# Attention, routed experts and SiLU layer on one core: PSUM as tiles of single banks, opened stage by stage, and one VectorE addition moved ahead of a transpose

## The chip, the cores and the metric

The kernel runs on one core of one Trainium2 chip. The core has five engines that each work through their own list of instructions: TensorE (matrix products, PE in the profile, with PEld for its weight loads), VectorE (DVE), ScalarE (ACT), GpSimd (POOL) and SyncE (SP, which issues transfers here). They wait for one another by semaphores. TensorE writes its products to PSUM, an accumulator memory of eight banks, each 512 float32 numbers on each of 128 partitions; VectorE and ScalarE read them from there. The metric is the time of one execution in microseconds (us) on the device, the median of several runs.

## The reference

Three layers follow one another; the output of each is the input of the next.

```python
# attention without softmax, B, S, D = 8, 3072, 256; z has 64 columns
scores = (1 / S) * np.matmul(z, z.transpose(0, 2, 1))
attn = np.maximum(scores, 0.0) ** 2
x = (u * np.matmul(attn, v)).reshape(B * S, D)
# routed experts: each of the 24576 tokens goes to one of E = 8
logits = normalized(x) @ normalized(expert_emb).T / tau
expert_idx = np.argmax(logits, axis=1)
out[mask_e] = gate_w[mask_e, None] * (np.maximum(x[mask_e] @ w1[e], 0) @ w2[e])
# the last layer, 256 -> 2048 -> 256
h = out @ w_in
return (h * (1 / (1 + np.exp(-h)))) @ w_out
```

## The kernel before

All products are made of float32 numbers cut into a high and a low part, so that one product of the reference is three matmuls here (high by high, high by low, low by high). The program is written out instruction by instruction in the order in which each engine executes it; nothing reorders it later. The semaphore waits are put in by the framework: an instruction that writes a tile waits for those that read it before.

**Stage A, the attention, with the router of the experts.** `pipeline_ab` runs over units g. A unit is a 512 by 256 piece of the scores. In the round of unit g TensorE makes the scores of unit g+2 (tile `s`), adds unit g to the output sums (`acc`), and then, since the scores are symmetric, adds a transposed copy of unit g-2 to the sums of another row block: `emit_T_a` makes that product in a bank of the tile `acct`, and one round later `flush_a` adds it on VectorE to the token rows `xg` (line 707). The tile `acct` has two banks; `ps_bank` hands them out in turn, to these transposed sums and also to the router, which makes its logits there (matmuls of lines 500 and 502). VectorE transposes the logits out of the bank (`raw`, line 507, tile `rt`) and adds their two parts (line 509). Jobs listed under `pre` run at the beginning of a round, `raw` among them; `bg` in its middle, `post` at its end.

**Stage B, the experts.** The same loop goes on with rounds of the experts' products; `ps_s` gives the two-bank tiles `s0` and `s1` in turn.

**Stage C, the last layer.** `pipeline_c` goes over 24 blocks of 1024 tokens (b) and in each over 8 groups of hidden columns (i), 192 iterations g = 8 b + i and one to drain. The first product is done by a Winograd form of Strassen's scheme: seven products M1 to M7, of three matmuls each (lines 1207 to 1209), give the four quadrants H11, H12, H21, H22. They go through four banks: `Q`, one of the two banks of the tile `m0` in turn, and `R` and `Z`, the two banks of the tile `m1`. M1 begins in Q, and M6, M5 and M3 are added onto it; M2 is made in R; M7 begins in Z and M4 is added onto it. Between two of these, ScalarE copies Q (`copy`, line 1264) or VectorE adds R or Z to a copy (`add`, line 1267, tile `hs`). ScalarE makes the sigmoid (`sig`, line 1270, tile `sg`), VectorE multiplies by it (`mul`, line 1273), ScalarE rounds the result (line 1279, tile `g`), and VectorE subtracts for the low part (line 1283). The multiplication for H12 reads Q itself, and is the last to read it: its row is `sg<-m,sg`. One iteration later TensorE multiplies the four quadrants by `w_out` into four banks `acc` (lines 1233 to 1235, two pairs of three matmuls for each quadrant, which makes 24 in an iteration). TensorE's order in an iteration is M1, M2, the H11 of the iteration before, M6, M7, H22, M5, H21, M3, M4, H12.

Between M7 and the subtraction for H11 comes what is to be done for the next block, one step for each i (`prep_c`): i=1 loads it, i=2 transposes, i=3 and 4 subtract, i=5, 6 and 7 cut 128x1024 numbers into parts (`split`: ScalarE line 151, VectorE line 152, tile `xp`), and i=0 cuts the last 128x512. In i=0 VectorE also takes the four finished `acc` of the block before out of PSUM (`evac_c`, line 1241).

Of the kernel before, what the change touches and what calls it, by code (L numbers as in the profile page):

```python
# [8 lines left out]
F32 = mybir.dt.float32  # L9
# [6 lines left out]
PSUM = bass.MemoryType.PSUM  # L16
# [4 lines left out]
def relu2_attention__moe_top1__silu_ffn_kernel(  # L21
# [24 lines left out]
    P = 128  # L46
# [34 lines left out]
    CH = CB // 2  # L81
# [3 lines left out]

    const = ctx.enter_context(tc.tile_pool(name="const", bufs=1))
    small = ctx.enter_context(tc.tile_pool(name="small", bufs=2))
    psS = ctx.enter_context(tc.tile_pool(name="psS", bufs=1, space=PSUM))
    psA = ctx.enter_context(tc.tile_pool(name="psA", bufs=4, space=PSUM))
    main = ctx.enter_context(tc.tile_pool(name="main", bufs=1))  # L90
    only_a = ExitStack()
    poolA = only_a.enter_context(tc.tile_pool(name="poolA", bufs=1))
# [14 lines left out]
    def pt(tag, shape, dtype, name, bufs):  # L107
        return poolA.tile(shape, dtype, tag=tag, name=name, bufs=bufs)
# [3 lines left out]
    sp_state = dict(n=0, bank=0, acct=None)  # L112

    def ps_s(shape, name):
        n = 0
        if sp_state["acct"] is None:
            n = sp_state["n"] % 2
            sp_state["n"] += 1
        return psS.tile(shape, F32, tag=f"s{n}", name=name, bufs=1)

    def ps_bank(n, name):

        if sp_state["acct"] is None:
            return ps_s([P, n], name)
        sp_state["bank"] ^= 1
        return sp_state["acct"][:, sp_state["bank"], 0:n]

    XS = nc.dram_tensor("xs_scratch", (E * CAP, XW), F32, kind="Internal").ap()
    X2 = nc.dram_tensor("x2_scratch", (N, D), F32, kind="Internal").ap()
# [92 lines left out]
    pre, bg, post = {}, {}, {}  # L222
# [10 lines left out]
    def run(tasks, g):  # L233
        for fn in tasks.pop(g, ()):
            fn()
# [38 lines left out]
    def both(g):  # L274

        return 0 <= g < NIT and UNITS[g][1] != UNITS[g][2]
# [4 lines left out]
    def start_a():  # L281

        for tag, n in (("tl", 1), ("vb", 2 * (NCH - 4)), ("xt0", 1), ("xt1", 1), ("xgh", 1), ("xgl", 1)):
            for _ in range(n):
                pt(tag, [P, 1024], F32, "place", n)
        sp_state["acct"] = psS.tile([P, 2, 512], F32, tag="s1", name="acct", bufs=1)
        low["zr"] = mt("w2", [P, 2, QN // 32, 32], F32, "zr", 4)

    jobs = []
# [386 lines left out]
    def th_a(g):  # L676
        h = TH[g] = (mt("y", [P, 8, 4, 32], F32R, "th", 1 - low["n"]) if g == NIT - 3
                     else mt("xh", [P, 8, 4, 32], F32R, "th"))
        A.activation(out=h, in_=TA[g].rearrange("p i k r -> p k i r"), func=AF.Copy)  # L679
# [24 lines left out]
    def flush_a(g):  # L704
        b, J, I, hf, _, _ = UNITS[g]
        x = XG[b, I][:, 2 * hf:2 * hf + 2, 0:D]
        V.tensor_tensor(out=x, in0=x, in1=TACC.pop(g), op=ALU.add)  # L707
# [248 lines left out]
    for b in range(NBLK):  # L956
        g = NIT + b * FP
# [9 lines left out]
    cw = {}  # L967
# [132 lines left out]
    def pipeline_ab():  # L1100

        g = min(bg)
        while g < NAB or bg:
            ahead = g + 2 if 0 <= g + 2 < NAB else None
            if g == NIT + 1:
                sp_state.update(acct=None, n=1)
            s = rest = None
            if ahead is not None:
                s = (emit_S_a if ahead < NIT else emit_S_b)(ahead)
            run(pre, g)  # L1110
            if both(g - 3):
                flush_a(g - 3)
            if both(g - 1):
                th_a(g - 1)
                tl_a(g - 1)
            if both(g + 1):
                ta_a(g + 1)
            run(bg, g)
            assert g not in pre
            if 0 <= g < NAB:  # L1120
                (emit_AV_a if g < NIT else emit_AV_b)(g)
            if both(g - 2):
                emit_T_a(g - 2)
            if s is not None:
                rest = (elem_a if ahead < NIT else elem_b)(ahead, s)
            if 0 <= g < NIT:
                if ahead >= NIT:
                    evac_a(g, range(QT))
                if rest:
                    rest()  # L1130
                run(post, g)
            else:
                run(post, g)
                if NIT <= g < NAB:
                    evac_b(g)
                if rest:
                    rest()
            g += 1
# [73 lines left out]
    quads, acc_c, out_c, room = {}, {}, {}, {}  # L1212
# [8 lines left out]
    def emit_AV_c(g, q):  # L1221

        b, i = divmod(g, GP)
        f, t = QUADS[q]
        x = quads.pop((g, q))
        start = i == 0 and q in ("H11", "H22")
        stop = i == GP - 1 and q in ("H21", "H12")
        for d in range(2):
            if start:
                acc_c[b, d, t] = psA.tile([P, CH], F32, tag="acc", name="acc")  # L1230
            o = acc_c[b, d, t]
            wh, wl = (cw["o"][:, f * GP + i, y, d * P:(d + 1) * P] for y in range(2))
            T.matmul(o, lhsT=wh, rhs=x[:, 0], start=start, stop=False)  # L1233
            T.matmul(o, lhsT=wh, rhs=x[:, 1], start=False, stop=False)  # L1234
            T.matmul(o, lhsT=wl, rhs=x[:, 0], start=False, stop=stop)  # L1235
# [11 lines left out]
                             in_=o[32 * i:32 * i + 32])  # L1247

    def pipeline_c():
        s0 = psS.tile([P, 2, CH], F32, tag="s0", name="m0", bufs=1)  # L1250
        s1 = psS.tile([P, 2, CH], F32, tag="s1", name="m1", bufs=1)
        ns = NCB * GP
        rooms_c()
        n_quad = 0
        H, C, S = room["H"], room["c"], room["a"]
        for g in range(ns + 1):
            now, old = g < ns, g > 0
            b, i = divmod(g, GP)
            end = old and i == 0
            todo = prep_c(b)[GP] if now and i == 0 else prep_c(b + 1)[i] if now and b + 1 < NCB else []  # L1260
            Q, R, Z = s0[:, g % 2], s1[:, 0], s1[:, 1]

            def copy(n, src):
                A.activation(out=C[n], in_=src, func=AF.Copy)

            def add(q, n, src):
                V.tensor_tensor(out=H[q], in0=src, in1=C[n], op=ALU.add)  # L1267

            def sig(q, src=None):
                A.activation(out=S[q], in_=H[q] if src is None else src, func=AF.Sigmoid)  # L1270

            def mul(q, src=None):
                V.tensor_tensor(out=S[q], in0=H[q] if src is None else src, in1=S[q], op=ALU.mult)  # L1273

            def high(g, q):
                nonlocal n_quad
                quads[g, q] = mt("hl"[n_quad % 2], [P, 2, CH], F32R, "g")
                n_quad += 1
                A.activation(out=quads[g, q][:, 0], in_=S[q], func=AF.Copy)  # L1279

            def low_part(g, q):
                x = quads[g, q]
                V.tensor_tensor(out=x[:, 1], in0=S[q], in1=x[:, 0].bitcast(F32), op=ALU.subtract)  # L1283

            if now:
                emit_M(g, "M1", Q)
            if old:
                high(g - 1, "H12")
                low_part(g - 1, "H22")
            if now:  # L1290
                copy(0, Q)
                emit_M(g, "M2", R)
            if old:
                low_part(g - 1, "H12")
                mul("H21")
                high(g - 1, "H21")
            if now:
                add("H11", 0, R)
            if old:
                low_part(g - 1, "H21")  # L1300
                emit_AV_c(g - 1, "H11")
            if now:
                sig("H11")
                mul("H11")
                emit_M(g, "M6", Q, False)
                copy(1, Q)
                high(g, "H11")
                emit_M(g, "M7", Z)
            for fn in todo:
                fn()  # L1310
            if now:
                low_part(g, "H11")
            if old:
                emit_AV_c(g - 1, "H22")
            if now:
                emit_M(g, "M5", Q, False)
                copy(2, Q)
            if old:
                emit_AV_c(g - 1, "H21")
            if now:  # L1320
                add("H22", 2, Z)
                sig("H22")
                emit_M(g, "M3", Q, False)
                emit_M(g, "M4", Z, False)
            if end:
                evac_c(b - 1, 0, 0)
            if now:
                sig("H12", Q)
                mul("H22")
                high(g, "H22")  # L1330
            if end:
                evac_c(b - 1, 0, 1)
            if now:
                add("H21", 1, Z)
                mul("H12", Q)
                sig("H21")
            if old:
                emit_AV_c(g - 1, "H12")
            if end:
                for d in range(2):  # L1340
                    evac_c(b - 1, 1, d)
# [51 lines left out]
```

## Time and profile before

| | before |
|---|---|
| median of 3 runs | 5296.63 us (5295.66 to 5301.29) |
| profiled execution | 5294.56 us |
| its span, first to last instruction | 5292.8 us |
| TensorE busy in it | 5180.2 us, 98% |
| VectorE busy | 4019.0 us, 76% |
| ScalarE busy | 3501.1 us, 66% |

Stage A takes the first 2055 us or so, stage B lasts to about 3190, stage C to the end. The profile is of one execution. A busy time is the time in which an instruction of that engine is drawn; since matmuls overlap one another, the rows of TensorE are longer than the distance from one to the next, and it is the distance that tells its rate.

### The profile page before, as it was taken

The numbers are of one execution on the slowest core, as the hardware profiler recorded it, in microseconds if no ns is written. First come the engines' busy times: TensorE is split into PE (matmuls) and PEld (weight loads), VectorE is DVE, ScalarE is ACT, GpSimd is POOL, SyncE is SP. The second block draws the span as 40 slices with busy tenths as digits, with TensorE's granted clock in tenths as the row PEclk, the third lists the DMA queues.
The fourth block names the chain that finished last, engine by engine and source line by source line (L and its number), as shares of the span: only waits on it lengthen the run. The fifth ranks groups of instructions, "written<-read, shape, count | busy, mean of one in ns | idle before, by whom it ended". The sixth has DMA issues, their size and how long they took to land.

```text
span 5292.8 us, 76091 instructions
## 1 busy us (share of the span) xinstructions
PE 5180.2 (98%) x27488; PEld 4389.7 (83%) x27488; DVE 4019.0 (76%) x5760; ACT 3501.1 (66%) x5213; POOL 750.0 (14%) x977
## 2 busy tenths in 40 slices
PE   8999999999999999999999998999999999999999
PEld 7889888898989898888888886777777777777777
DVE  6687777777777778788877676777777777777776
ACT  7777777777777776555555555666666666666665
POOL 1131313222222222211111110000000000000000
PEclk9999999999999999999999998999999999999999
DMA  4555565656565656755555551101101010101010
GB/s 148 176 169 181 169 184 163 186 160 183 169 178 169 180 172 185 196 159 160 160 147 160 152 170 41 33 20 29 29 20 32 17 32 17 32 17 32 17 32 17
DMA packets 789371, 594.31 MB, mean 112 GB/s; under 512 B 473692, under 2 KB 706175, under 8 KB 788992
## 3 DMA queue, kind: packets, MB, share of 16 engines
q1 hardware_dynamic: 616960, 464.93, 29.7%
q10 hardware_dynamic: 152928, 73.95, 5.4%
q0 software_dynamic: 19104, 50.56, 2.6%
q8 instruction: 215, 3.52, 0.3%
q14 instruction: 164, 1.34, 0.1%
HBM read 368.03 MB, written 210.73 MB: 109 GB/s over the span
## 4 chain that ended last, share of the span: by engine, by line
PE 65%; issue 11%; DVE 9%; ACT 6%; DMA 6%; POOL 1%; SPq 1%; ACTq 0%; POOLq 0%; DVEq 0%
PE acc L242 6%; PE acc L239 6%; PE m L1207 5%; PE m L1209 4%; PE m L1208 4%; PE acc L1234 4%; PE acc L1233 4%; PE acc L1235 4%; PE acct L700 4%; PE acct L701 4%; PE acct L702 4%; PE acc L241 3%; PE acc L240 3%; PE s L645 2%; PE s L646 2%
## 5 line engine op out<-in xcount | busy, mean ns | idle before, releaser
L1233 PE MATMUL acc<-g,wo 128*128 128x512 f32 x1536 | 598.9, 390 | 0.0
L1234 PE MATMUL acc<-g,wo 128*128 128x512 f32 x1536 | 598.2, 389 | 0.2 <-DVE g L1283 0.2
L1235 PE MATMUL acc<-g,wo 128*128 128x512 f32 x1536 | 597.7, 389 | 0.0
L1279 ACT ACTIVATE g<-sg 128x512 fp32r<-128x512 f32 x768 | 484.1, 630 | 133.2 <-DVE sg L1273 120.2
L1283 DVE TENSOR_TENSOR g<-sg,g 128x512 fp32r<-128x512 f32 x768 | 524.4, 685 | 59.1 <-ACT g L1279 23.9
L700 PE MATMUL acct<-vs,th 128*128 128x256 f32 x1920 | 542.6, 283 | 15.3 <-DVE xg L707 14.4
L701 PE MATMUL acct<-vs,th 128*128 128x256 f32 x1920 | 541.8, 282 | 0.0
L702 PE MATMUL acct<-vs,tl 128*128 128x256 f32 x1920 | 541.4, 282 | 0.0
L242 PE MATMUL acc<-vs,ah 128*128 128x512 f32 x1344 | 533.5, 397 | 0.0
L239 PE MATMUL acc<-vs,ah 128*128 128x512 f32 x1344 | 533.1, 397 | 0.0
L1270 ACT ACTIVATE sg<-hs 128x512 f32<-128x512 f32 x576 | 364.2, 632 | 202.6 <-DVE hs L1267 194.0
L667 DVE TENSOR_TENSOR al<-a,ah 128x1024 fp32r<-128x1024 f32 x336 | 406.2, 1209 | 109.8 <-ACT ah L660 105.0
L1273 DVE TENSOR_TENSOR sg<-hs,sg 128x512 f32<-128x512 f32 x576 | 395.9, 687 | 120.9 <-ACT sg L1270 118.7
L654 ACT ACTIVATE a<-s 128x1024 f32<-128x1024 f32 x336 | 342.5, 1019 | 183.1 <-PE s L646 164.2
L930 ACT ACTIVATE hh<-hps 128x1024 fp32r<-128x1024 f32 (+1 forms) x220 | 213.9, 972 | 336.6 <-PE hps L916 289.3
L931 DVE SCALAR_TENSOR_TENSOR hl<-hps,hh 128x1024 fp32r<-128x1024 f32 (+1 forms) x220 | 254.1, 1155 | 204.9 <-ACT hh L930 202.2
L679 ACT ACTIVATE th<-at 128x1024 fp32r<-128x1024 f32 x240 | 253.4, 1056 | 230.7 <-PE acct L701 130.2
L665 DVE STREAM_TRANSPOSE tb<-a 128x1024 f32<-128x1024 f32 x240 | 297.5, 1240 | 133.1 <-ACT a L656 130.3
L700 PEld LDWEIGHTS acct<-vs,th 128*128 128x128 f32 x1920 | 364.9, 190 | 18.8 <-DVE xg L707 17.6
L241 PE MATMUL acc<-vs,al 128*128 128x256 f32 x1344 | 375.4, 279 | 0.0
L701 PEld LDWEIGHTS acct<-vs,th 128*128 128x128 f32 x1920 | 365.6, 190 | 10.2
L240 PE MATMUL acc<-vs,al 128*128 128x256 f32 x1344 | 374.1, 278 | 0.0
(246 smaller groups left out, 14006.1 us busy)
## 6 DMA issues: line engine op xcount, KB each, us to landing
ts_scratch<-tb SPq DMA_DIRECT2D x240, 512.0 KB
at<-ts_scratch SPq DMA_DIRECT2D x960, 128.0 KB
r<-in_moe_w_dram SPq DMA_DIRECT2D x220, 512.0 KB
vr<-in_v_dram ACTq DMA_DIRECT2D x48, 512.0 KB
ut<-in_u_dram ACTq DMA_DIRECT2D x48, 512.0 KB
xb<-xs_scratch SPq DMA_DIRECT2D x192, 128.0 KB
xc<-x_scratch SPq DMA_DIRECT2D x192, 128.0 KB
out_dram<-oc SPq DMA_DIRECT2D x192, 128.0 KB
```

Source lines behind the costliest of these rows:

```text
L239: T.matmul(acc, lhsT=hs[0], rhs=ws[0], start=start, stop=False)
L240: T.matmul(acc[:, D:2 * D], lhsT=ls[0], rhs=ws[0][:, 0:D], start=False, stop=False)
L241: T.matmul(acc[:, D:2 * D], lhsT=ls[1], rhs=ws[1][:, 0:D], start=False, stop=False)
L242: T.matmul(acc, lhsT=hs[1], rhs=ws[1], start=False, stop=stop)
L700: T.matmul(acc[:, kk], lhsT=lh, rhs=vq[:, 0], start=(q == 0), stop=False)
L701: T.matmul(acc[:, kk], lhsT=lh, rhs=vq[:, 1], start=False, stop=False)
L702: T.matmul(acc[:, kk], lhsT=ll, rhs=vq[:, 0], start=False, stop=(q == QT - 1))
L1233: T.matmul(o, lhsT=wh, rhs=x[:, 0], start=start, stop=False)
L1234: T.matmul(o, lhsT=wh, rhs=x[:, 1], start=False, stop=False)
L1235: T.matmul(o, lhsT=wl, rhs=x[:, 0], start=False, stop=stop)
L1279: A.activation(out=quads[g, q][:, 0], in_=S[q], func=AF.Copy)
L1283: V.tensor_tensor(out=x[:, 1], in0=S[q], in1=x[:, 0].bitcast(F32), op=ALU.subtract)
```

## The change

PSUM's pools are opened and closed with the stages. In stage A the two banks of the transposed sums are two tiles `t0` and `t1` of one bank each; at the beginning of stage B they are given up and the two-bank tile `s1` is opened in a pool of its own; at the beginning of stage C all of these are closed and eight tiles of one bank each are opened, four (`m0` to `m3`) for Q twice, R and Z, and four for the output sums, with a fixed name for each. In the attention's round, the addition `flush_a` is issued ahead of the jobs in `pre`. The diff, whole:

```diff
--- before.py
+++ after.py
@@ -85,8 +85,10 @@
 
     const = ctx.enter_context(tc.tile_pool(name="const", bufs=1))
     small = ctx.enter_context(tc.tile_pool(name="small", bufs=2))
-    psS = ctx.enter_context(tc.tile_pool(name="psS", bufs=1, space=PSUM))
-    psA = ctx.enter_context(tc.tile_pool(name="psA", bufs=4, space=PSUM))
+    not_c, in_a = ExitStack(), ExitStack()
+    psS = not_c.enter_context(tc.tile_pool(name="psS", bufs=1, space=PSUM))
+    psA = not_c.enter_context(tc.tile_pool(name="psA", bufs=4, space=PSUM))
+    psT = in_a.enter_context(tc.tile_pool(name="psT", bufs=1, space=PSUM))
     main = ctx.enter_context(tc.tile_pool(name="main", bufs=1))
     only_a = ExitStack()
     poolA = only_a.enter_context(tc.tile_pool(name="poolA", bufs=1))
@@ -116,14 +118,14 @@
         if sp_state["acct"] is None:
             n = sp_state["n"] % 2
             sp_state["n"] += 1
-        return psS.tile(shape, F32, tag=f"s{n}", name=name, bufs=1)
+        return (sp_state["psB"] if n else psS).tile(shape, F32, tag=f"s{n}", name=name, bufs=1)
 
     def ps_bank(n, name):
 
         if sp_state["acct"] is None:
             return ps_s([P, n], name)
         sp_state["bank"] ^= 1
-        return sp_state["acct"][:, sp_state["bank"], 0:n]
+        return sp_state["acct"][sp_state["bank"]][:, 0:n]
 
     XS = nc.dram_tensor("xs_scratch", (E * CAP, XW), F32, kind="Internal").ap()
     X2 = nc.dram_tensor("x2_scratch", (N, D), F32, kind="Internal").ap()
@@ -283,7 +285,7 @@
         for tag, n in (("tl", 1), ("vb", 2 * (NCH - 4)), ("xt0", 1), ("xt1", 1), ("xgh", 1), ("xgl", 1)):
             for _ in range(n):
                 pt(tag, [P, 1024], F32, "place", n)
-        sp_state["acct"] = psS.tile([P, 2, 512], F32, tag="s1", name="acct", bufs=1)
+        sp_state["acct"] = [psT.tile([P, 512], F32, tag=f"t{i}", name="acct", bufs=1) for i in range(2)]
         low["zr"] = mt("w2", [P, 2, QN // 32, 32], F32, "zr", 4)
 
     jobs = []
@@ -1103,13 +1105,15 @@
         while g < NAB or bg:
             ahead = g + 2 if 0 <= g + 2 < NAB else None
             if g == NIT + 1:
-                sp_state.update(acct=None, n=1)
+                in_a.close()
+                psB = not_c.enter_context(tc.tile_pool(name="psB", bufs=1, space=PSUM))
+                sp_state.update(acct=None, n=1, psB=psB)
             s = rest = None
             if ahead is not None:
                 s = (emit_S_a if ahead < NIT else emit_S_b)(ahead)
-            run(pre, g)
             if both(g - 3):
                 flush_a(g - 3)
+            run(pre, g)
             if both(g - 1):
                 th_a(g - 1)
                 tl_a(g - 1)
@@ -1227,7 +1231,7 @@
         stop = i == GP - 1 and q in ("H21", "H12")
         for d in range(2):
             if start:
-                acc_c[b, d, t] = psA.tile([P, CH], F32, tag="acc", name="acc")
+                acc_c[b, d, t] = cw["ps"].tile([P, CH], F32, tag=f"acc{2 * t + d}", name="acc", bufs=1)
             o = acc_c[b, d, t]
             wh, wl = (cw["o"][:, f * GP + i, y, d * P:(d + 1) * P] for y in range(2))
             T.matmul(o, lhsT=wh, rhs=x[:, 0], start=start, stop=False)
@@ -1247,8 +1251,9 @@
                              in_=o[32 * i:32 * i + 32])
 
     def pipeline_c():
-        s0 = psS.tile([P, 2, CH], F32, tag="s0", name="m0", bufs=1)
-        s1 = psS.tile([P, 2, CH], F32, tag="s1", name="m1", bufs=1)
+        not_c.close()
+        ps = cw["ps"] = ctx.enter_context(tc.tile_pool(name="psC", bufs=1, space=PSUM))
+        banks = [ps.tile([P, CH], F32, tag=f"m{i}", name="m", bufs=1) for i in range(4)]
         ns = NCB * GP
         rooms_c()
         n_quad = 0
@@ -1258,7 +1263,7 @@
             b, i = divmod(g, GP)
             end = old and i == 0
             todo = prep_c(b)[GP] if now and i == 0 else prep_c(b + 1)[i] if now and b + 1 < NCB else []
-            Q, R, Z = s0[:, g % 2], s1[:, 0], s1[:, 1]
+            Q, R, Z = banks[g % 2], banks[2], banks[3]
 
             def copy(n, src):
                 A.activation(out=C[n], in_=src, func=AF.Copy)
```

Line numbers after the change are higher by 2 in the attention and by 4 in stage C. On each of the five engines the instructions are as many as before and, apart from 15 places on VectorE, in the same order. Three places show what moves.

VectorE in the attention, where the router's logits have just been made; `xg<-xg,acct` is the addition of `flush_a`, `rt` and `raw` are the router's. Before:

```order
L667 TENSOR_TENSOR al<-a,ah 128x1024 [waits Activation_49]
L507 STREAM_TRANSPOSE rt<-acct 128x256 [waits PE_49]
L509 TENSOR_TENSOR raw<-rt 128x64 [waits DVE_49]
L707 TENSOR_TENSOR xg<-xg,acct 128x2x256
L684 TENSOR_TENSOR tl<-at,th 128x1024 [waits DMAHW4_49,DMAHW3_49,DMAHW7_49,DMAHW1_49,Activation_49]
```

and after:

```order
L669 TENSOR_TENSOR al<-a,ah 128x1024 [waits Activation_49]
L709 TENSOR_TENSOR xg<-xg,acct 128x2x256 [waits PE_49]
L509 STREAM_TRANSPOSE rt<-acct 128x256 [waits PE_49]
L511 TENSOR_TENSOR raw<-rt 128x64 [waits DVE_49]
L686 TENSOR_TENSOR tl<-at,th 128x1024 [waits DMAHW4_49,DMAHW3_49,DMAHW7_49,DMAHW1_49,Activation_49]
```

The addition stands ahead of the router's two instructions. This is so at 15 places.

TensorE in stage C, at the end of one iteration and the beginning of the next, where M1 (three matmuls) and M2 are made; before, they write `m0` and `m1`:

```order
L1235 MATMUL acc_35801<-g_35839,wo_24236 128x512
L1207 MATMUL m0_35698<-xp_35678,wih_24234 128x512 [waits DVE_49]
L1208 MATMUL m0_35698<-xp_35679,wih_24234 128x512
L1209 MATMUL m0_35698<-xp_35678,wil_24235 128x512
L1207 MATMUL m1_35699<-xp_35678,wih_24234 128x512
L1208 MATMUL m1_35699<-xp_35679,wih_24234 128x512
L1209 MATMUL m1_35699<-xp_35678,wil_24235 128x512
```

and after, two tiles of one bank each, both named `m`:

```order
L1239 MATMUL acc_35817<-g_35855,wo_24244 128x512
L1211 MATMUL m_35713<-xp_35686,wih_24242 128x512
L1212 MATMUL m_35713<-xp_35687,wih_24242 128x512
L1213 MATMUL m_35713<-xp_35686,wil_24243 128x512
L1211 MATMUL m_35714<-xp_35686,wih_24242 128x512
L1212 MATMUL m_35714<-xp_35687,wih_24242 128x512
L1213 MATMUL m_35714<-xp_35686,wil_24243 128x512
```

The order is the same; the wait for VectorE at M1 is gone. M7 and M4 have one before and after.

TensorE at an early transposed sum of the attention, behind the output sums of the round. Before:

```order
L241 MATMUL acc<-vs,al 128x256
L242 MATMUL acc<-vs,ah 128x512
L700 MATMUL acct<-vs,th 128x256 [waits DVE_49]
L701 MATMUL acct<-vs,th 128x256
L702 MATMUL acct<-vs,tl 128x256
```

and after:

```order
L243 MATMUL acc<-vs,al 128x256
L244 MATMUL acc<-vs,ah 128x512
L702 MATMUL acct<-vs,th 128x256
L703 MATMUL acct<-vs,th 128x256
L704 MATMUL acct<-vs,tl 128x256
```

Here too only a wait for VectorE is gone. At 101 of the 240 transposed sums the first matmul no longer has one.

## Rows read from the trace of the kernel before

**Rows 1.** The page, busy us of each engine (share of the span) and its instructions.

```profile
PE 5180.2 (98%) x27488; PEld 4389.7 (83%) x27488; DVE 4019.0 (76%) x5760; ACT 3501.1 (66%) x5213; POOL 750.0 (14%) x977
```

**Rows 2.** TensorE's waits: line <- released by: us in total, times, longest us.

```profile
PE m L1207 <- DVE sg L1273: 32.1, 93, 1.4
...
PE acct L700 <- DVE xg L707: 14.4, 10, 1.8
...
PE acct L500 <- DVE xg L707: 2.1, 1, 2.1
```

**Rows 3.** Windows: us, busy us of PE, PEld, DVE, ACT, POOL; granted clock; DMA share, GB/s.

```profile
3301.00:5259.00 1958.00, 1925.85 (x8192) 1516.37 (x8190) 1526.02 (x2317) 1266.45 (x2093) 0.00 (x0) 1.00 0.10 25
2060.00:3190.00 1130.00, 1126.17 (x5888) 963.58 (x5887) 861.97 (x1275) 619.71 (x961) 245.49 (x240) 1.00 0.57 163
3215.00:3222.00 7.00, 5.67 (x12) 3.52 (x13) 4.83 (x7) 3.36 (x7) 0.00 (x0) 0.50 0.37 84
```

**Rows 4.** Timeline of TensorE, one block: M1s, and in i=2 M6 and H12.

```profile
4334.31 0.50 PE L1207 MATMUL m<-xp,wih 128*128 128x512 f32 x1 [0.25 <-DVE sg L1273]
...
4345.38 0.50 PE L1207 MATMUL m<-xp,wih 128*128 128x512 f32 x1 [0.58 <-DVE sg L1273]
...
4356.10 0.50 PE L1207 MATMUL m<-xp,wih 128*128 128x512 f32 x1
...
4358.97 0.39 PE L1207 MATMUL m<-xp,s 128*128 128x512 f32 x1
...
4365.09 0.39 PE L1233 MATMUL acc<-g,wo 128*128 128x512 f32 x1
...
4387.69 0.50 PE L1207 MATMUL m<-xp,wih 128*128 128x512 f32 x1
...
4398.59 0.50 PE L1207 MATMUL m<-xp,wih 128*128 128x512 f32 x1 [0.25 <-DVE sg L1273]
...
4420.40 0.50 PE L1207 MATMUL m<-xp,wih 128*128 128x512 f32 x1 [0.26 <-DVE sg L1273]
```

**Rows 5.** Timeline of three engines in i=6 of the same block.

```profile
4397.86 0.68 DVE L1273 TENSOR_TENSOR sg<-m,sg 128x512 f32<-128x512 f32 x1
...
4401.84 0.68 DVE L1273 TENSOR_TENSOR sg<-hs,sg 128x512 f32<-128x512 f32 x1
...
4402.32 0.60 ACT L1264 ACTIVATE c<-m 128x512 f32<-128x512 f32 x1 [0.52 <-PE m L1209]
4402.82 0.62 ACT L1279 ACTIVATE g<-sg 128x512 fp32r<-128x512 f32 x1
4403.34 1.05 ACT L151 ACTIVATE xp<-xs 128x1024 fp32r<-128x1024 f32 x1
...
4406.17 0.68 DVE L1267 TENSOR_TENSOR hs<-m,hs 128x512 f32<-128x512 f32 x1
...
4406.91 0.50 PE L1207 MATMUL m<-xp,wih 128*128 128x512 f32 x1
...
4408.76 0.68 DVE L1273 TENSOR_TENSOR sg<-m,sg 128x512 f32<-128x512 f32 x1
```

**Rows 6.** Timeline of VectorE and TensorE at two places of the attention.

```profile
259.01 0.44 DVE L507 STREAM_TRANSPOSE rt<-acct 128x256 f32<-128x256 f32 x1
259.48 0.91 DVE L509 TENSOR_TENSOR raw<-rt 128x64 f32<-128x64 f32 x1
260.32 0.67 DVE L707 TENSOR_TENSOR xg<-xg,acct 128x512 f32<-128x512 f32 x1
...
261.04 0.38 PE L700 MATMUL acct<-vs,th 128*128 128x256 f32 x1 [1.57 <-DVE xg L707]
...
808.93 0.39 PE L700 MATMUL acct<-vs,th 128*128 128x256 f32 x1 [1.84 <-DVE xg L707]
```

**Rows 7.** Timeline of TensorE near the beginning of stage C.

```profile
3209.21 0.63 PE L1207 MATMUL m<-xp,wih 128*128 128x512 f32 x1
3209.63 0.63 PE L1208 MATMUL m<-xp,wih 128*128 128x512 f32 x1
```

## The prediction

> **What bounds the kernel now.** I read the page's busy shares first. TensorE is busy for 5180.2 of 5292.8 us [rows 1], so whatever the change does to the time it must do through TensorE, and only about 2% looks free. That share hides something, because a matmul held back by a semaphore is drawn longer, not idle. So I went on to TensorE's waits. The longest group is the first matmul of a product in the last stage (stage C), waiting for a VectorE multiplication `sg`; in the attention, the transposed sums wait for VectorE's addition to `xg` ten times [rows 2].
>
> Then I put the stages side by side [rows 3]. The middle stage has matmuls for 1126.17 of 1130 us. The steady part of stage C, from 3301 to 5259 us, has 8192 matmul records in 1958.00 us, 0.239 us each. What one costs when nothing holds it is seen inside an iteration: from the first matmul of M6 at 4358.97 to the first of the `H12` pair at 4365.09 there are 27 matmuls in 6.12 us, 0.2267 us each [rows 4]. An iteration has 45 matmuls (seven products of 3, eight of the output side of 3), so it would take 10.20 us; 1958.00 over 8192/45 = 182 iterations is 10.76. TensorE loses 0.56 us in each, 106 us in 192, though its row says 98% busy.
>
> Where it loses them: M1, the first product. It writes bank g%2 of the tile `m0`, whose last reader is two iterations back. Yet it starts at 4398.59, 0.05 us after the multiplication `sg<-m` of the iteration before (4397.86 + 0.68 = 4398.54), which reads the other bank [rows 4, 5]. So the wait is for the whole two-bank tile. Held this way, the matmul is drawn with 0.50 us instead of 0.39: the next one starts 0.11 us later than usual, which is a second price of every hold [rows 4].
>
> **The change part by part.** *Single-bank tiles in stage C.* M1 loses its wait on VectorE in 191 of 192 iterations, as the order of the program shows; M7 now waits for the last reader of its own bank, an addition of the iteration before, and no longer for one in `m1`'s other half. Instruction counts and orders stay as they are on all five engines except for VectorE's swap below, so no duration changes; only what is waited for does. What M1 gives up must be checked against what is late next. VectorE and ScalarE keep up with the rate on average (1526 and 1266 us busy in the 1958 [rows 3]), but M4 adds onto the bank that the addition `hs<-m,hs` has just read, and keeps that wait.
>
> I take a block of eight iterations, one block of tokens, from M1 to M1 [rows 4]: i=0 (four evacuations of `acc`) 4334.31 to 4345.38, 11.07 us; i=1 10.72; i=2 to 4 31.59 for three; i=5 10.90; i=6 and 7 21.81. In all 86.09.
> - i=0 and i=2 to 4: M4 there is not late now (i=2: its 27 undisturbed matmuls above contain M4). Without the hold at M1 they run at TensorE's own 10.20.
> - i=1: here M7 is late as well, behind the evacuations on VectorE. That wait is the other-bank kind and goes too; the evacuations still push ScalarE's copies towards M5. Nothing shows how far, from 0 up to what an ordinary iteration loses, 0.33. I take 0.15, near the middle: 10.35.
> - i=5 to 7 prepare the next block: ScalarE rounds 128x1024 and VectorE subtracts, between the copy of M6 and the addition that M4 waits for. [Rows 5] show the chain in i=6. From multiplication to multiplication (`sg<-m`, 4397.86 to 4408.76) it takes 10.90 us, and I followed it link by link: `sg<-hs` ends at 4402.52; ScalarE copies M6 (`c<-m` 4402.32) and so starts `g` only at 4402.82; `xp` on ScalarE, then on VectorE `xp`, `g` and `hs<-m,hs` to 4406.85, M4 at 4406.91. M4 is barely late now (0.03, and 0.11 for the hold). All links but one are VectorE's and ScalarE's own. The one is the copy, which is tied to TensorE: with TensorE ahead it lies earlier, and `g` can follow the multiplication by the 0.05 us or so that hand-overs here take, at 4402.57, 0.25 earlier. The chain is then 10.65 us against TensorE's 10.20. So in i=6 and 7 most of what M1 gave up **comes back at M4**, and the iteration takes 10.66; in i=5 TensorE comes out of ordinary iterations with VectorE's lag small, and M4 loses what it loses now: 10.20 + 0.14 = 10.34.
>
> Sum: 10.20 + 10.35 + 30.60 + 10.34 + 21.32 = 82.81, against 86.09: 3.28 a block, 78.7 in 24 blocks. The last block prepares nothing and gains 8 x 0.33 = 2.6 instead, and the first iterations run at the lower clock [rows 7], where TensorE is slower than VectorE's chain: I take off 1.7 for both, the second by choice. **Stage C: -77 us.** Its bounds: 0 if the hold stays, 106 if no wait is left.
>
> *Single-bank tiles and the swap in the attention.* Ten holds of the transposed sums come to 14.4 us, one of the router's sums to 2.1 [rows 2]. Seven of the ten look like the one at 261.04 [rows 6]: VectorE does the transpose `rt` (259.01), the addition `raw` (259.48, 0.91 long) and only then the addition to `xg` (260.32), and TensorE, which has been waiting for 1.57 us, goes on 0.05 after it. In the changed order the addition to `xg` comes first. But at this place the router has used one of the two banks in between, so the sum goes to the bank that `rt` reads. It then waits for 0.67 + 0.44 from 259.01, to about 260.17: 0.87 is won, 6.1 us in seven. The other three (808.93 is the longest, 1.84 [rows 6]) wait for an addition that reads the other bank; they go, 3.4 us together, and so does the router's 2.1, each with its 0.11. **Attention: -12 us**, bounds 0 (ScalarE, whose reads TensorE waits for at other places, takes it back) and 18 (all of it). Moving `rt` and `raw` behind one addition of 0.67 us delays the routing by that much, 15 times; nothing on TensorE waits for `raw` within its iteration. VectorE's new waits for TensorE at `xgl` and `bb` name reads and sums that their data always needed, and cost nothing. Opening pools anew costs no instruction; the waits at the two stage borders are for the same last readers as before.
>
> The sum is made against the profiled execution, 5294.56 us with 1.76 us around its span: 5294.6 - 77 - 12 = 5205.6. The runs' median is 2.1 above that execution; I put 1.4 on it: **5207 us**.
>
> **Rivals.**
> - *Nothing comes back.* Perfetto Trace Analysis, the Trainium skill's page, section Optimizing Tensor Performance, asks that independent groups of matmuls rotate through different PSUM banks, so that reading one out overlaps the next group; by it, all of the wait should go. M1, M2 and M7 then are such groups, M4 is not. Time if M4's holds also went: 5294.6 - 106 - 12 = 5177. For it: the chain in [rows 5] has ScalarE steps that could close up further. Against it: M4 adds onto a bank that VectorE must have read.
> - *More comes back.* If the chain of VectorE and ScalarE binds in all eight iterations, each wins only the 0.25 of the copy: 48 us, and half of the attention's: 5294.6 - 48 - 6 = 5241. Against it: in an ordinary iteration VectorE and ScalarE have no preparation to do.
> - *Slower: the clock.* With the holds moved, TensorE could be granted its lower level in stage C. It stands at 0.50 of full speed (1.2 of 2.4 GHz) after the wait at the stage's beginning, and there matmuls come 0.43 us apart, not 0.23 [rows 3, 7]. An iteration at that level is 45 x 0.43 = 19.4, 9.2 more; ten of them undo the gain, and a quarter of the stage (48) gives 5205.6 + 440 = 5646. Against it: a hold in every iteration of stage C left the clock at 1.00 for 1958 us, and the middle stage, denser than stage C will be, had 1.00 too [rows 3]. TensorE: Matmul & The Clock Gate in the Trainium skill tells, under A second HAM failure mode, of a kernel that cycled through banks and idled briefly between groups until its clock swung between both levels; the trace of before does not agree so far, since just such idling went by at 1.00.
> - *The change doesn't do what it says.* M1's place waits for something else, such as the weights or the next block's parts. Then only the attention gains: 5283; with that absorbed too, 5295.
>
> **How the numbers follow.** Chances: my forecast 0.58 (own range 5192 to 5222), nothing comes back 0.13, more comes back 0.19, no effect 0.06 (half of it within 0.2%), slower 0.04. The range that holds 8 in 10 reaches to the two nearest rivals: 5174 to 5244. 0.2%, some 10.6 us, is about what a measurement of this kernel can tell from no change. Faster by more: 0.58 + 0.13 + 0.19 + 0.03 = 0.93; within: 0.03; slower 0.04.
>
> **What would show it.** After the change, TensorE's waits should have no M1 row for `sg`, and rows of M4 for the addition `hs` should grow to some 0.35 us in i=6 and 7, two in a block of eight. Steady stage C should take about 82.8 us a block, and stage C's ordinary iterations 10.2. In the attention, seven holds of 0.6 to 0.7 us behind `rt` should be left. I am wrong if ordinary iterations stay above 10.35 (then the chain binds where I saw none), if M4's rows stay as they are (then 5207 is too high), or if the granted clock drops in stage C.

## The result and the profile after

The changed kernel takes 5207.46 us (median of 4 runs, 5206.43 to 5210.27). Beside it the kernel before took 5298.15 (4 runs, 5295.66 to 5301.29). The ratio is 0.9829, 95% interval 0.9812 to 0.9846. The profiled execution took 5207.61 us, its span is 5205.9.

The page's busy shares, answering to [rows 1]:

```profile
PE 5130.2 (99%) x27488; PEld 4403.7 (85%) x27488; DVE 4016.5 (77%) x5760; ACT 3501.9 (67%) x5213; POOL 759.3 (15%) x977
```

The instruction counts are the same to the last one, and VectorE and ScalarE work as long as before. TensorE's busy time is 50 us shorter, though no work was removed: a matmul is drawn 0.39 us long and the next starts after 0.23, so a short hold is covered by a drawn matmul and counts as busy. TensorE's waits, answering to [rows 2] (us in total, times, longest; all lines of code stand 2 to 5 lower down than before):

```profile
PE s L647 <- ACT a L656: 15.0, 9, 2.8
...
PE acct L702 <- DVE rt L509: 5.5, 7, 1.7
...
PE m L1211 <- DVE hs L1272: 4.9, 29, 0.5
PE m L1211 <- ACT c L1269: 4.8, 2, 4.6
PE acct L502 <- ACT xgh L153: 3.3, 4, 1.7
```

The row of 93 waits for `sg` is gone. In its place stand 29 for the addition `hs`; 28 of them are M4 in i=6 and 7. In the attention, ten waits for `xg` (14.4 us) and the router's one (2.1) have become seven for `rt` (5.5), and four for ScalarE's `xgh` show (3.3; before, there was one of 0.4). The window of steady stage C, answering to [rows 3] (us, busy us of PE, PEld, DVE, ACT, POOL, granted clock, DMA share, GB/s):

```profile
3285.00:5172.00 1887.00, 1880.50 (x8197) 1531.28 (x8196) 1526.97 (x2318) 1268.40 (x2094) 0.00 (x0) 1.00 0.11 26
```

1887.00 over 8197/45 = 182.2 iterations is 10.36 us each; it was 10.76. VectorE's and ScalarE's work is squeezed into 71 us less, and the granted clock is at 1.00. TensorE's timeline of one block, answering to [rows 4]; the M1s are those of i=0, 1, 2, 5, 6, 7 and the next i=0:

```profile
4281.83 0.39 PE L1211 MATMUL m<-xp,wih 128*128 128x512 f32 x1
...
4292.03 0.39 PE L1211 MATMUL m<-xp,wih 128*128 128x512 f32 x1
...
4297.52 0.50 PE L1211 MATMUL m<-xp,wih 128*128 128x512 f32 x1
...
4302.44 0.39 PE L1211 MATMUL m<-xp,wih 128*128 128x512 f32 x1
...
4333.04 0.39 PE L1211 MATMUL m<-xp,wih 128*128 128x512 f32 x1
...
4343.46 0.39 PE L1211 MATMUL m<-xp,wih 128*128 128x512 f32 x1
...
4351.93 0.50 PE L1211 MATMUL m<-xp,wih 128*128 128x512 f32 x1 [0.15 <-DVE hs L1272]
...
4354.11 0.39 PE L1211 MATMUL m<-xp,wih 128*128 128x512 f32 x1
...
4364.75 0.39 PE L1211 MATMUL m<-xp,wih 128*128 128x512 f32 x1
```

Every M1 is drawn with 0.39 now: none is held. The 0.50 marks where the holds went, M5 in i=1 (4297.52) and M4 in i=6 (4351.93). The block takes 82.92 us. Means over the steady iterations, i=0 to 7: 10.20, 10.40, 10.20, 10.20, 10.20, 10.42, 10.65, 10.65.

VectorE's and ScalarE's timeline in i=6, answering to [rows 5]:

```profile
4343.14 0.68 DVE L1278 TENSOR_TENSOR sg<-m,sg 128x512 f32<-128x512 f32 x1
...
4347.12 0.69 DVE L1278 TENSOR_TENSOR sg<-hs,sg 128x512 f32<-128x512 f32 x1
...
4351.20 0.68 DVE L1272 TENSOR_TENSOR hs<-m,hs 128x512 f32<-128x512 f32 x1
...
4353.79 0.68 DVE L1278 TENSOR_TENSOR sg<-m,sg 128x512 f32<-128x512 f32 x1
...
4347.06 0.60 ACT L1269 ACTIVATE c<-m 128x512 f32<-128x512 f32 x1
4347.84 0.63 ACT L1284 ACTIVATE g<-sg 128x512 fp32r<-128x512 f32 x1 [0.18 <-DVE sg L1278]
4348.38 1.04 ACT L153 ACTIVATE xp<-xs 128x1024 fp32r<-128x1024 f32 x1
```

From multiplication to multiplication it takes 4353.79 - 4343.14 = 10.65. ScalarE's copy ends at 4347.66, before the multiplication `sg<-hs` does (4347.81), and `g` follows the multiplication, not the copy. M4 starts 0.05 after the addition ends at 4351.88.

VectorE and TensorE at one of the seven places of the attention, answering to [rows 6]:

```profile
507.95 0.68 DVE L709 TENSOR_TENSOR xg<-xg,acct 128x512 f32<-128x512 f32 x1
508.55 0.44 DVE L509 STREAM_TRANSPOSE rt<-acct 128x256 f32<-128x256 f32 x1
509.02 0.32 DVE L511 TENSOR_TENSOR raw<-rt 128x64 f32<-128x64 f32 x1
...
509.04 0.38 PE L702 MATMUL acct<-vs,th 128*128 128x256 f32 x1 [0.63 <-DVE rt L509]
```

TensorE goes on 0.05 after `rt`; the hold is 0.63, no longer 1.57.

### The profile page after: what moved, and what is told of

The parts are those of the page before. It is cut to its first block, busy times and chain, and to the rows that moved or that the text cites. A ratio compares the mean times of both kernels' runs of the same rounds, so it can differ in the third digit from the quotient of the medians.

```text
span 5205.9 us, 76118 instructions
## 1 busy us (share of the span) xinstructions
PE 5130.2 (99%) x27488; PEld 4403.7 (85%) x27488; DVE 4016.5 (77%) x5760; ACT 3501.9 (67%) x5213; POOL 759.3 (15%) x977
## 4 chain that ended last, share of the span: by engine, by line
PE 68%; issue 9%; DVE 8%; ACT 8%; DMA 6%; POOL 1%; SPq 1%; ACTq 0%; POOLq 0%; DVEq 0%
PE acc L244 6%; PE acc L241 6%; PE acc L1239 5%; PE acc L1237 5%; PE acc L1238 5%; PE m L1211 4%; PE m L1213 4%; PE m L1212 4%; PE acct L702 4%; PE acct L703 4%; PE acct L704 4%; PE acc L243 3%; PE acc L242 3%; ACT g L1284 2%; PE s L647 2%
```

## The experiments

Each one is compared with the kernel before on the same chip. Executions of one kernel lie 4 to 13 us apart, so differences of a few us are read from traces, not from times.

**Stage C alone (e1).** The attention keeps its two-bank tile and VectorE's old order:

```diff
-        return sp_state["acct"][sp_state["bank"]][:, 0:n]
+        return sp_state["acct"][:, sp_state["bank"], 0:n]
 ...
-        sp_state["acct"] = [psT.tile([P, 512], ...) for i in range(2)]
+        sp_state["acct"] = psT.tile([P, 2, 512], ...)
 ...
+            run(pre, g)
             if both(g - 3):
                 flush_a(g - 3)
-            run(pre, g)
```

> Single-bank tiles in stage C alone; the attention keeps its two-bank tile and its order. My theory (stage C and the attention gain separately): 5298 - 78 = 5220 us, stage C's blocks of eight iterations at about 82.9 us, and the attention's ten waits for the addition to xg are all there, 14.4 us. Rival (the pools' new places in PSUM, or both edits together, make the gain): over 5235 us, or blocks above 84 us.

Measured: 5218.8 us (5214.17 to 5222.51), ratio 0.9847 (0.9831 to 0.9864). The blocks are those of the whole change (10.20, 10.42, 10.20, 10.20, 10.20, 10.42, 10.65, 10.65), and ten waits for `xg` are back, 13.5 us. Stage C's banks are worth 79.7 us of the 91.

**The attention alone (e2).** The opposite half: stage C keeps `m0` and `m1`, each of two banks.

```diff
-        banks = [ps.tile([P, CH], ..., tag=f"m{i}") for i in range(4)]
+        s0 = ps.tile([P, 2, CH], F32, tag="s0", name="m0", bufs=1)
+        s1 = ps.tile([P, 2, CH], F32, tag="s1", name="m1", bufs=1)
 ...
-            Q, R, Z = banks[g % 2], banks[2], banks[3]
+            Q, R, Z = s0[:, g % 2], s1[:, 0], s1[:, 1]
```

> The attention's single banks and the swap alone; stage C with its two-bank tiles as before. Theory: the attention's part of the gain adds to that of stage C: the changed kernel less the one with stage C alone is 5207.5 - 5218.8 = -11.3, so 5298.3 - 11 = 5287, with blocks in stage C of 86.1 us. Rival: the attention's part is only the 8.7 us that stage C starts earlier in one profile: 5289.5. Rival: opening the pools anew for stage C is what gains there, and not the single banks: below 5230.

Measured: 5285.52 us (5280.62 to 5290.45), beside 5299.51 before; ratio 0.997 (0.996 to 0.9981), 14 us with an interval of some 5 either way. The iterations in stage C are those of before, 10.53 to 11.08. Its pools are opened anew here too, so that alone gains nothing. The halves add up: 79.7 + 14.0 = 93.7 against 90.7 for the whole.

**Only M1's tile split (e3).** Bank g%2 is a tile of its own; R and Z share one of two banks.

```diff
-        banks = [ps.tile([P, CH], ..., tag=f"m{i}") for i in range(4)]
+        banks = [ps.tile([P, CH], ..., tag=f"m{i}") for i in range(2)]
+        s1 = ps.tile([P, 2, CH], F32, tag="s1", name="m1", bufs=1)
 ...
-            Q, R, Z = banks[g % 2], banks[2], banks[3]
+            Q, R, Z = banks[g % 2], s1[:, 0], s1[:, 1]
```

> The changed kernel, with Q's two banks as two tiles but R and Z again as one tile of two banks. My theory: M1's hold came from the tile of Q, so M1 stays free; M7 must wait for the addition that reads R in its own iteration, which ends 0.4 us or more before M7 is due except in i=1, where it ends 0.9 us late: i=1 takes about 11.2 us instead of 10.4, all others as in the changed kernel, 5207 + 24 x 0.85 = 5227 us. Rival (each tile carries half of the gain): about 5250 us, with M7 held in most iterations.

Measured: 5228.9 us (5224.01 to 5230.76), ratio 0.9868 (0.9851 to 0.9884). Seven iterations of the block are those of the whole change; i=1 takes 11.28. The timeline in that iteration, VectorE's addition H11 and M7:

```profile
4307.22 0.68 DVE L1273 TENSOR_TENSOR hs<-m,c 128x512 f32<-128x512 f32 x1
...
4307.95 0.50 PE L1211 MATMUL m<-xp,s 128*128 128x512 f32 x1 [0.78 <-DVE hs L1273]
```

M7 writes Z and waits for the addition that reads R. The evacuations push that addition back only in i=1; the second tile's split is worth 0.88 there, once a block, and nothing elsewhere in steady stage C.

**Where M1's hold went: the preparation moved (e4).** If M4 is held in i=5 to 7 because the next block's parts stand ahead of the addition H22 on ScalarE and VectorE, they can be issued behind it:

```diff
+            late = now and i > 4
-            for fn in todo:
+            for fn in () if late else todo:
                 fn()
 ...
                 add("H22", 2, Z)
+                for fn in todo if late else ():
+                    fn()
```

> The changed kernel, with the cutting into parts in i=5 to 7 issued behind the addition that M4 waits for. My theory: the holds of M4 there (about 0.2, 0.45 and 0.45 us a block) are what M1's hold turned into, and they go: 23 x 1.1 = 25 us, 5207 - 25 = 5182 us, i=5 to 7 at 10.2 us each. Rival (VectorE and ScalarE bind as a whole in these three iterations, wherever the parts stand): the holds turn up at another product, 5195 to 5207 us.

Measured: 5183.44 us (5180.76 to 5191.06), ratio 0.9782 (0.9766 to 0.9798). i=5, 6 and 7 take 10.20, and TensorE's waits for `hs` are gone from steady stage C. The M1s of i=5 and of the next i=0, three iterations apart, in one block:

```profile
4326.06 0.39 PE L1211 MATMUL m<-xp,wih 128*128 128x512 f32 x1
...
4356.66 0.39 PE L1211 MATMUL m<-xp,wih 128*128 128x512 f32 x1
```

i=1 grew from 10.40 to 10.57, which over the stage gives back some 4 of the 26 us that i=5 to 7 gain. Its timeline, VectorE's read-outs of the finished block (`oc`), ScalarE's copy of M6 and M5:

```profile
4285.69 1.29 DVE L1245 STREAM_TRANSPOSE oc<-acc 128x512 f32<-128x512 f32 x2
...
4288.68 0.68 DVE L1272 TENSOR_TENSOR hs<-m,c 128x512 f32<-128x512 f32 x1
...
4289.40 0.64 ACT L1275 ACTIVATE sg<-hs 128x512 f32<-128x512 f32 x1
...
4289.94 0.58 ACT L1269 ACTIVATE c<-m 128x512 f32<-128x512 f32 x1
...
4290.57 0.50 PE L1211 MATMUL m<-xp,wih 128*128 128x512 f32 x1
```

Two read-outs delay the addition H11 (4288.68), ScalarE's sigmoid waits for the addition, the copy stands behind the sigmoid, and M5 follows the copy by 0.05.

**Both read-outs behind that addition (e5).** With the parts moved as in e4:

```diff
                 add("H11", 0, R)
+            if now and g > 1 and i == 1:
+                for d in range(2):
+                    evac_c(b - 1, 1, d)
 ...
-            if end:
+            if end and not now:
                 for d in range(2):
                     evac_c(b - 1, 1, d)
```

> As the run before it, and the last two evacuations of a block are issued in i=1 behind the addition that reads R instead of at the end of i=0. My theory: M5's hold in i=1 (0.2 us) comes from ScalarE's copy behind these evacuations and goes: 24 x 0.2 = 5 us more, 5177 us, every iteration at 10.2 us. Rival: the output sums of H22 then wait for their banks, due 4.1 us into i=1, and the time is 5182 us or above.

Measured: 5184.04 us (5180.05 to 5190.3), ratio 0.9786 (0.9769 to 0.9802): the theory missed, and the rival holds. M5 is free, yet i=1 takes 10.50. The timeline of the same place:

```profile
4282.59 1.30 DVE L1245 STREAM_TRANSPOSE oc<-acc 128x512 f32<-128x512 f32 x2
...
4283.44 0.47 PE L1237 MATMUL acc<-g,wo 128*128 128x512 f32 x1
...
4283.97 0.40 PE L1239 MATMUL acc<-g,wo 128*128 128x512 f32 x1
4284.00 0.19 PEld L1237 LDWEIGHTS acc<-g,wo 128*128 128x128 f32 x1
4284.21 0.40 PE L1237 MATMUL acc<-g,wo 128*128 128x512 f32 x1
```

At 4283.44 H22's output products open the new block's sums, in the banks that the two transposes read (4282.59 to 4283.89). That is the reader that the rival named. The matmul is held 0.16, and drawn 0.47.

**One read-out on each side (e8).** With the parts moved as in e4, the first at the end of i=0, the second behind the addition H11 of i=1:

```diff
+            if now and g > 1 and i == 1:
+                evac_c(b - 1, 1, 1)
 ...
             if end:
-                for d in range(2):
-                    evac_c(b - 1, 1, d)
+                evac_c(b - 1, 1, 0)
+                if not now:
+                    evac_c(b - 1, 1, 1)
```

> As e4 (parts of i=5 to 7 behind the addition H22), but of the four transposes that read out a finished block only the last one (row half 1, output half 1) is moved into the next iteration, behind the addition H11. Theory: in i=1 two things wait for VectorE's read-outs from opposite sides. With both at the end of i=0 (e4), the addition H11 is 1.3 us later and M5 is held behind ScalarE's copy (iteration 10.57); with both behind H11 (e5) the products H22 of the new block find their two banks not yet read and are held (10.50). With one on each side neither is late: i=1 takes 10.20 to 10.25, and the time is that of e4, 5183.4, less 24 x 0.35 = 5175. Rival: i=1 is late because of what the iterations before leave over, wherever the read-outs stand: i=1 stays at 10.45 or more, and the time at 5181 to 5184.

Measured: 5178.55 us (5176.38 to 5182.62), ratio 0.9773 (0.9759 to 0.9786). The M1s of i=0, 1 and 2 in one block:

```profile
4265.50 0.39 PE L1211 MATMUL m<-xp,wih 128*128 128x512 f32 x1
...
4275.72 0.39 PE L1211 MATMUL m<-xp,wih 128*128 128x512 f32 x1
...
4285.92 0.39 PE L1211 MATMUL m<-xp,wih 128*128 128x512 f32 x1
```

On average i=1 takes 10.22, i=0 10.23, the others 10.20: the mechanism held and the rival fell. The time is 3.5 us over the expected one. In the profiles stage C is 8.4 shorter than in e4, 0.9 of it in the first iteration; the medians, of two chips, differ by 4.9, within their scatter.

**The swap alone, in the kernel before (e6).**

```diff
-            run(pre, g)
             if both(g - 3):
                 flush_a(g - 3)
+            run(pre, g)
```

> The kernel before with the swap alone; all tiles of two banks. Theory A: the sums wait for the last VectorE reader of the whole tile. That was xg, behind rt and raw; with the swap it is rt, directly behind xg, so seven holds shrink from 1.57 to 0.65 and the others stay: 5298.3 - 6.4 = 5292. Rival B: the order on VectorE changes nothing, because both reads have to be done either way: 5298 and holds of 1.4 to 1.6.

Measured: 5294.17 us (11 runs, 5290.19 to 5300.4), ratio 0.9992 (0.9983 to 1.0001): the time decides nothing. TensorE's waits in the attention do:

```profile
PE acct L700 <- DVE xg L707: 6.1, 6, 1.6
...
PE acct L700 <- DVE rt L507: 3.8, 6, 0.6
PE acct L500 <- DVE xg L707: 3.3, 1, 3.3
```

Six of the seven holds are of some 0.63 behind `rt` now, as theory A has it. But six for `xg` are left with 6.1 us, where theory A left three, and the router's one grew from 2.1 to 3.3: of 16.5 us [rows 2] 13.2 remain. The other 3.3 came back too: the waits for ScalarE's `a` grew from 14.6 us to 17.8, and all of TensorE's waits in the first 2060 us come to 50.7, against 50.6 before. So theory A is right about these holds, but in this profile, of an execution of 5299.06 us, what they gave up came back as other waits. Why the others grew is open.

**The change without the swap (e7).** The diff of the swap above, reversed, in the changed kernel.

> The changed kernel with VectorE's order as it was (rt and raw ahead of the addition to xg), banks single everywhere. Theory A: with single banks the seven held sums wait for rt alone, because they are written to the bank that rt reads; the swap puts an addition of 0.63 us ahead of rt, so without it the seven holds shrink from 0.63 to about 0.05, and the time is 5207.5 - 4.2 = 5203. Rival B: the sums wait for the addition to xg still, and the swap is worth here what it was forecast to be worth, 0.87 us a hold: 5207.5 + 6 = 5213.5, with holds of 1.5.

Measured: 5207.45 us (5201.68 to 5210.62), ratio 0.9824 (0.9811 to 0.9838). Rival B (5213.5) is over the highest run. VectorE and TensorE at the first of the seven places:

```profile
258.91 0.44 DVE L509 STREAM_TRANSPOSE rt<-acct 128x256 f32<-128x256 f32 x1
259.38 0.93 DVE L511 TENSOR_TENSOR raw<-rt 128x64 f32<-128x64 f32 x1
260.23 0.68 DVE L709 TENSOR_TENSOR xg<-xg,acct 128x512 f32<-128x512 f32 x1
...
259.40 0.39 PE L702 MATMUL acct<-vs,th 128*128 128x256 f32 x1
```

The sum starts 0.05 after `rt`, with no wait listed, while `xg` is still 0.83 away. Of the waits for `rt` one is left, of 1.2 us. So theory A is right about the wait. The medians are equal, and stage C begins 2.1 us earlier in the profiles (3196.10 against 3198.23). With the run below that makes two profiles without the swap, 3193.30 and 3196.10, and the six of single banks with it begin stage C at 3198.23 to 3202.53: a sign that the swap costs a few us here, which the medians don't confirm.

**Both ends (e9).** The read-outs and parts as in e8, without the swap.

> The edits to stage C of e8 (5178.55) together with VectorE's old order in the attention (rt and raw ahead of the addition to xg, as in e7). In e7 the seven holds of the transposed sums were gone from the trace, yet the median stayed that of the changed kernel. If stage C has no wait left and the attention's holds of 0.63 are real time on TensorE, 2 to 4 us come off: 5175 to 5177, with 10.20 in the iterations of stage C and no row of seven waits for rt. Rival: what the holds give up goes into TensorE's waits for the exponentials on ScalarE at the next scores, as the unchanged median of e7 suggests: 5178.5, and the row of waits for ScalarE's a grows by some 3 us.

Measured: 5176.3 us (5169.77 to 5179.77), ratio 0.9764 (0.9751 to 0.9777), the fastest of all kernels here, though not separable from the 5178.55. The waits of the seven places are gone, and TensorE's waits for ScalarE's `a` in the attention (20 to 2055 us) are 11.4 us, as in e8 (11.6): the rival is not borne out.

## Why the prediction was right, point by point

**What bounds the kernel.** Right: a floor of 0.2267 us a matmul, 10.20 an iteration, is what every iteration reaches, to within 0.03, once its holds are gone (e8). The whole tile as the cause of M1's hold is shown: splitting that tile alone (e3 beside e2) brought seven of eight iterations to their new times.

**Stage C, -77 us.** Measured 78.2: the span shrank by 86.9, and stage C's first M1 starts at 3198.23, 8.7 earlier than the 3206.93 of before. By iteration:
- i=0 and i=2 to 4: 10.20 forecast, 10.20 measured.
- i=1: 10.35 forecast, with 0.15 chosen; 10.40 measured. The way of the delay is as forecast, evacuations to ScalarE's copy to M5.
- i=5: 10.34 forecast, 10.42 measured, the largest miss of the block. I let M4 lose what it lost before. The traces show what that left out (means of 21 blocks): with M1 no longer drawn out by a hold, M4 would start 8.16 after M1, 0.11 earlier than before, but the addition ends only 0.07 earlier, 8.19 after M1 instead of 8.26. So M4 is 0.09 late, and not 0.02, beside the 0.11 of a hold.
- i=6 and 7: 10.66 forecast, 10.65 measured. The chain's one link tied to TensorE closed as worked out, and the chain takes 10.65.
- The block: 82.81 forecast, 82.92 measured; a block gains 3.15 in place of 3.28.
- The beginning: the first two iterations gained 4.1 (18.29 to 15.68 and 12.03 to 10.53), where I had taken time off, by choice. In the changed kernel the half clock ends earlier. Windows of the kernel before, 15 to 21 us after its first M1, and of the changed one, 14 to 24 us after:

```profile
3222.00:3228.00 6.00, 4.62 (x12) 3.12 (x11) 3.87 (x6) 3.85 (x7) 0.00 (x0) 0.50 0.34 76
...
3212.00:3222.00 10.00, 9.52 (x41) 7.20 (x40) 8.10 (x13) 6.40 (x12) 0.00 (x0) 1.00 0.23 52
```

The granted clock is 0.50 in the first and 1.00 in the second. Why it rose earlier is not shown; all eight kernels with Q's banks split have a first iteration of 15.66 to 16.58, all three others 18.29. In sum the first block gained 6.0, the 22 after it 69.2, the last 3.0. That 77 came so close to 78.2 is thus partly luck: about 3 us too much for the blocks and nearly 4 too little for the beginning offset each other.

**Comes back at M4** was the step that carried the forecast, and the moved preparation shows it: with the parts behind the addition the three iterations take 10.20. So what M4 loses is set by the work ahead of the addition that reads its bank. The sign that I gave for it, rows of some 0.35 us, two in a block, was wrong: the list has 28 rows of some 0.16. In i=6 and 7 M4 does start 0.31 late, but half of that lies under the matmul drawn before it, and the list leaves it out.

**The attention, -12 us.** In times 14.0 alone, 11.3 with stage C done (5218.8 - 5207.46); 8.7 in one pair of profiles. The size is right within what can be told. Of the seven holds forecast six came, of 0.62 to 0.64. The seventh row, of 1.73, is another: it stands at 2023.7, in the round where the router waited 2.1 before (2021.5). So the router's 2.1, which I had let go, mostly came back. And the attribution failed in one step: "0.87 is won" was credited to the banks and the swap together. Without the swap those holds shrink to nothing. With banks of their own the sums wait for `rt` alone, and the swap puts an addition of 0.6 us ahead of it; it shortens holds only where `xg` and `rt` share a tile, and there e6 shows no shorter time beyond the noise. The waits for `xgh`, which no term held, come to 3.3 us in this profile and to 0.8 to 2.7 in those of the experiments.

**The rivals.** *Nothing comes back* (5177) failed for this change, and its time was reached by the last two kernels. Perfetto Trace Analysis in the Trainium skill, Optimizing Tensor Performance, asks that independent groups rotate through banks; the trace agrees for them: in steady stage C, M1, M2 and M7 have no wait left. The same sentence notes that an accumulation group targets one bank by construction; M4, which adds onto M7's bank, is such a case. There the order of VectorE's and ScalarE's work had to change (10.65 to 10.20). *More comes back* (5241) fell with 10.20 in four of eight iterations. *The clock* stayed at 1.00 in steady stage C. *No effect* fell.

## What to carry to other kernels

When a hold goes, follow the chain of the engines behind it and ask which instruction is late next; here TensorE won 4% of an iteration, and the next limit was work of ScalarE and VectorE that merely stood ahead of a needed read and could be moved, at the price of 0.17 us in one other iteration of the block. An order that shortened a wait on a shared tile should be looked at again once the tile is split: here it then lengthened the wait. Before a read-out is moved, list both sides that wait for it, the instructions queued behind it and the next writer of the bank it reads.

## What the runs showed of the hardware

- A hold has a second price that the list of waits leaves out: a matmul of 128x512 behind one is drawn with 0.50 us instead of 0.39, and the next starts 0.34 after it instead of 0.23 (4351.93 to 4352.27). The product before had its last matmul at 4351.39, so M4 comes 0.54 after it, 0.31 late; with the 0.11 that is 0.42 of the 0.45 that the iteration loses. The wait listed is 0.15.
- The addition `raw` (128x64), which adds two parts of `rt`, is drawn with 0.23 us at 17 of its 24 places. At the other seven, those of the seven holds, it is drawn with 0.90 to 0.92 in the kernel before and 0.31 to 0.34 in the changed one. At just these seven GpSimd (POOL) subtracts 128x512 numbers; here in the kernel before and in the changed one:

```profile
259.04 1.27 POOL L152 TENSOR_TENSOR vs<-vr,vs 128x512 fp32r<-128x512 f32 x1 [1.03 <-ACT vs L151]
...
507.98 1.27 POOL L154 TENSOR_TENSOR vs<-vr,vs 128x512 fp32r<-128x512 f32 x1 [1.04 <-ACT vs L153]
```

The subtraction ends at 260.31 and 509.25, and `raw` at 260.39 [rows 6] and 509.34. In all eleven profiles `raw` ends 0.08 after it at each of the seven places, while the addition `xg`, which reads a bank of PSUM, is drawn with 0.67 to 0.69 beside it. So `raw` seems to wait for GpSimd, and 0.68 of the hold of 1.57 is that wait. No run moved the subtraction, so this is argued from the times.
- Executions of one kernel differ by up to 13 us (5294.62 to 5307.59 over 18 of the kernel before), and stage C's start in the profiles of kernels with the same attention from 3198.2 to 3202.5. Terms of a few us in the first two stages can't be told apart by time here, only by their waits.
